# Attention through agents, then one expert per token: a first batch whose keys all come ahead of its values in float32, maxima without GpSimd, and an expert picked from a mean

## The chip, the cores and the metric

The kernel runs on one core of one Trainium2 chip. The metric is the time of the whole program on the device in microseconds (us), lower is better: the median of 3 runs, 1204.39 us for the kernel before (1203.04 to 1204.79). A core has TensorE (PE in the profile; PEld is its weight loads), VectorE (DVE), ScalarE (ACT), GpSimd (POOL) and SyncE (SP, which here only starts DMAs). Each takes its instructions in order, and semaphores hold one engine until another is done.

## The reference

Four batches of 11,456 tokens with 128 features, and 49 agents per batch. First the agents look at all keys, then each query looks at the 49 agents, and the result goes through the best of 8 experts:

```python
def sm(a, b):                               # scores, softmax
    s = scale * (a @ b.transpose(0, 2, 1))
    s = s - s.max(-1, keepdims=True)
    e = np.exp(s)
    return e / (e.sum(-1, keepdims=True) + 1e-09)
agent_v = sm(agents, k) @ v                 # 4 x 49 x 128
x = (sm(q, agents) @ agent_v).reshape(B * N, 128)
xn = x / (norm(x) + 1e-06); en = expert_emb / (norm(expert_emb) + 1e-06)
logits = xn @ en.T / tau                    # 8 experts
expert_idx = np.argmax(logits, axis=1)      # top 1
gate_w = softmax(logits)[chosen]
out[token] = gate_w * (np.maximum(x[token] @ w1[e], 0) @ w2[e])   # 128 -> 1024 -> 128
```

So the values of a batch can only be weighted once its keys have been scored, and no query of a batch gets to its expert before that batch's `agent_v` is done.

## The kernel before

A batch is cut into 12 units of 1,024 tokens (128 partitions by 8 chunks; the last unit has 2 chunks of 96 tokens). Scores have 49 columns per chunk.

**Precision.** PE multiplies f16 at full rate, so an f32 operand is split into a f16 high part and a f16 low part. `split` does it for a unit of keys or queries: ACT squares it for a scale (L284), then high and low parts are made. In the FFN phase `LO_BY` deals out the low part: for "d" ACT makes the high part (L291) and DVE the low part (L296); for "P" POOL makes the high part (L289) and DVE the low part; for "p" ACT makes the high part and POOL the low part in two instructions (L293, L294). A DMA transposes both (L299, issued by SP), and three products per chunk make the scores (L308 to L310). Half the key units of the first batch go another way, `k1_f32`: PE transposes the f32 unit itself (L356) and multiplies in f32 (L365).

**One batch.** `k1_unit` and `k1_f32` score keys and keep a running maximum in `m_run` (L342, L368). `k_max` reduces it on DVE (L399) and across the 128 partitions by `allred`, a partition_all_reduce on POOL (L135). `k2_unit` takes the exponential of the scores less the maximum (L382, L384) and multiplies with the values and a column of ones (`avp`, L388, 129 columns, f32). `av_chain` adds up (`foldp`, L424, L426) and leaves `avT` (L432), the agents' values. `q_unit` does the softmax of a query unit (L545 to L554), has its weights transposed by DMA (`tt`, L556) and multiplies them with `r_hi`, `r_lo` (L565, L566), which yields the logits of the experts.

**Experts.** Nearly all tokens of a batch choose the same expert. The kernel counts votes among the tokens of the batch's first query unit (`pick_expert`), loads that expert's weights (L529, L530), folds `agent_v` into `w1` (`gh`, `gl`) and runs the batch's feed-forward part (FFN) with it. Tokens that chose another expert are counted (`count_strays`, L135 again) and done apart at the end.

**FFN.** 23 tiles per batch of 512 tokens, 8 steps per tile, so 184 steps per batch and 736 in all. A step: `hp` from `tt` and `gh`, `gl` (L698, L699, 512 columns), ACT's relu to f16 (L702), DVE's low part `hl` (L703), and three products with `w2` per 128 tokens (L720 to L722). `ot` (L735) goes out by DMA (L741).

**Order.** `first` is the start of the program: `PAT` lists its work for batch 0 letter by letter (K and V units, m for `k_max`, q for a query unit, c for `av_chain`), and `AHEAD` says how many letters ahead loads are issued. Then the FFN loop runs, and between its steps the generators `keys` (keys and values of batches 1 to 3, in the windows `W_`, as shares of 184 steps: keys from, keys to, values from, values to) and `queries` put in the work of what is to come. A scheduler then sets each engine's order; SP's DMAs stand in the order of the code at the start.

Of the kernel before, what the change touches and what calls it, by code (L numbers as in the profile page):

```python
# [10 lines left out]
F16 = mybir.dt.float16  # L11
# [20 lines left out]
def kernel(ctx: ExitStack, tc: tile.TileContext, q, k, v, agents, emb, tau, w1, w2, out):  # L32
# [23 lines left out]

    LO_BY = {"k": "pdP", "q": "pP"}
    LAG = 4

# [8 lines left out]
    ld = ctx.enter_context(tc.tile_pool(name="ld", bufs=8))  # L68
# [51 lines left out]
    unit_load(k, "k", 0, 0)  # L120
    a_sb = sm.tile([A, B, C], F32, name="a_sb", tag="a_sb", bufs=1)
    sp.dma_start(out=a_sb, in_=agents.rearrange("b a c -> a b c"))
    unit_load(k, "k", 0, 1)
    ident = cst.tile([P, P], F32, name="ident")
    make_identity(nc, ident)
# [48 lines left out]
    def now_run(g):  # L174

        while True:
            try:
                next(g)
            except StopIteration as s:
                return s.value  # L180

# [3 lines left out]
    sga, isga = now_run(pow2(allred(amx, 1, "amxr"), 10, "sga"))  # L185
# [7 lines left out]
    eights = cst.tile([P, P], BF16, name="eights")  # L193
    half = cst.tile([P, GC], F32, name="half")
    iota_k = cst.tile([P, E], BF16, name="iota_k")
# [34 lines left out]
    def setup():  # L230
# [47 lines left out]
    def split(kind, b, u, g):  # L278
# [4 lines left out]
        xs = wk.tile([P, UJ, 2, D], F16, name=kind + "s", tag="xs", bufs=3)  # L283
# [14 lines left out]
        xT = wk.tile([P, 2 * UJ, P], F16, name=kind + "T", tag="xT", bufs=3)  # L298
# [15 lines left out]
    def k_start(b):  # L314
# [3 lines left out]
        for us in [range(x, y) for x, y in zip(e, e[1:])]:  # L318
# [3 lines left out]
            pool.memset(kb.m_run, -3.0e38)  # L322
# [5 lines left out]
    def k1_unit(b, u, g, cp):  # L328
# [8 lines left out]
        if cp is act:  # L337
            act.activation(st, spv, AF.Copy, scale=iv)
        else:
            dve.tensor_scalar(st, spv, iv, None, ALU.mult)  # L340
        yield g[2]
        dve.tensor_tensor(out=kb.m_run[:p, :n, :], in0=kb.m_run[:p, :n, :], in1=st, op=ALU.max)  # L342
        kb.s[u] = st
        kb.k1 += 1

    def k1_f32(b, u):
# [15 lines left out]
        yield 1  # L362
# [4 lines left out]
        act.activation(st, s[:p, : n * A].rearrange("p (c a) -> p c a", a=A), AF.Copy, scale=sga[:p])  # L367
        dve.tensor_tensor(out=kb.m_run[:p, :n, :], in0=kb.m_run[:p, :n, :], in1=st, op=ALU.max)  # L368
# [27 lines left out]
    def k_max(b, i=0):  # L396
# [3 lines left out]
        kb.m = allred(m1, A, "kmax", bufs=max(2, NB))  # L400
# [15 lines left out]
    def av_chain(b, g):  # L416
# [8 lines left out]
        for i, (x, m) in enumerate(fm):  # L425
# [8 lines left out]
                          in1=lr.unsqueeze(1).broadcast_to([P, 2, A]), op=ALU.mult)  # L434
        yield g
# [24 lines left out]
    def pick_expert(b, zo, g):  # L460
# [4 lines left out]
        n = ushape(0)[1]  # L465
        psx = pss if b else psh
        key = psx("key")
        for c in range(n):
            pe.matmul(out=key[:, :E], lhsT=eights, rhs=zo[:, c, :], start=(c == 0), stop=False)
        pe.matmul(out=key[:, :E], lhsT=eights, rhs=iota_k, start=False, stop=True)  # L470
        e0i = sm.tile([P, 1], I32, name="e0i", tag="e0i")
        dve.tensor_reduce(out=e0i, in_=key[:, :E], axis=AX.X, op=ALU.max)
        yield 1
# [4 lines left out]
        yield 5  # L478
        gh = wk.tile([P, F], F16, name="gh", tag="gh")
# [56 lines left out]
    def q_unit(b, u, g):  # L536
        bt = batches[b]
        p, n = ushape(u)
        while ("q", b, u) not in units:
            yield 1  # L540
        xT, iv = yield from split("q", b, u, g[0])
        yield g[1]
        spv = scores(b, u, xT)
# [12 lines left out]
        sp.dma_start_transpose(out=tt[:, : n * p].rearrange("k (c p) -> k c p", p=p),  # L556
                               in_=e2[:p, :n, :].rearrange("p c k -> p (c k)"))
# [553 lines left out]
```

## Time and profile before

| | |
|---|---|
| Median of 3 runs | 1204.39 us |
| Profiled execution: its time / span of the core | 1205.41 / 1203.6 us |
| Mean granted TensorE clock | 0.958 |
| Busy: PE / PEld / DVE / ACT / POOL | 86 / 70 / 75 / 57 / 36% |
| First FFN product (L698) starts | 109.56 us |
| L703 (`hl`, DVE) | 736 times, 475.5 us |
| L720, L721, L722 (PE) | 2880 times each, 222 ns mean |

The shares are means over the start (up to 110 us, no FFN) and the FFN phase. The page's slices show what a mean hides: a slice of 30 us with a low PE digit or a low clock digit has a wait in it.

### The profile page before, as it was taken

The page shows a single profiled execution, that of the slowest core. Times are in us where ns is not written, and L with a number is a line of the kernel's source. Part 1 is how long each engine was busy: PE and PEld are TensorE (multiplying, and loading weights), DVE is VectorE, ACT ScalarE, POOL GpSimd, SP SyncE. Part 2 cuts the span into 40 slices and gives each one's busy share as a digit, 9 for nine tenths or more (in the row PEclk, how much of TensorE's full clock was granted, in tenths as well). Part 3 has the DMA queues.
Part 4 walks back from the last instruction along what each step waited for, and adds up shares of the span by engine and source line. Part 5 has one row for each costly group of instructions (what it writes and reads, how often), then busy time and mean ns, then how long its engine had stood idle before and what let it go on. Part 6 is the DMA issues. An engine that isn't in the chain of part 4 may idle for free. (4 is left out here: it accounts for less than half of the span.)

```text
span 1203.6 us, 34100 instructions
## 1 busy us (share of the span) xinstructions
PE 1036.3 (86%) x13877; PEld 844.2 (70%) x13877; DVE 903.1 (75%) x2103; ACT 686.9 (57%) x1304; POOL 430.0 (36%) x409
## 2 busy tenths in 40 slices
PE   2666876698999877799998987689999989999998
PEld 2664655577787765587887776568788867877776
DVE  2555787567688896788778887686778998777785
ACT  2434676455647765555755676555554575655553
POOL 2002665445401644733442343733331262252200
PEclk9887898899999999899999999899999999999999
DMA  4976999465225988554542699753330382241100
GB/s 143 249 143 209 226 200 206 106 159 128 68 60 199 205 202 192 123 119 111 140 137 54 151 236 204 158 98 96 100 73 28 91 208 68 93 92 46 39 37 32
DMA packets 302697, 157.35 MB, mean 131 GB/s; under 512 B 227067, under 2 KB 279371, under 8 KB 302539
## 3 DMA queue, kind: packets, MB, share of 16 engines
q1 hardware_dynamic: 302475, 155.16, 54.4%
q8 instruction: 109, 1.79, 0.6%
q14 instruction: 49, 0.40, 0.1%
q0 software_dynamic: 64, 0.00, 0.0%
HBM read 75.80 MB, written 23.53 MB: 83 GB/s over the span
## 5 line engine op out<-in xcount | busy, mean ns | idle before, releaser
L703 DVE SCALAR_TENSOR_TENSOR hl<-hp,hh 128x512 f16<-128x512 f32 (+1 forms) x736 | 475.5, 666 | 95.9 <-ACT hh L702 86.2
L702 ACT ACTIVATE hh<-hp 128x512 f16<-128x512 f32 (+1 forms) x736 | 414.8, 584 | 217.0 <-PE yp L721 95.1
L720 PE MATMUL yp<-w2h,hh 128*128 128x128 f16 (+1 forms) x2880 | 528.5, 222 | 6.2 <-DVE ot L735 6.2
L721 PE MATMUL yp<-w2l,hh 128*128 128x128 f16 (+1 forms) x2880 | 529.0, 222 | 1.9 <-DVE w2l L516 1.9
L722 PE MATMUL yp<-w2h,hl 128*128 128x128 f16 (+1 forms) x2880 | 528.8, 222 | 0.0
L698 PE MATMUL hp<-tt,gh 128*128 128x512 f16 (+1 forms) x736 | 277.8, 378 | 66.1 <-DVE hl L703 60.4
L720 PEld LDWEIGHTS <-hh 128*128 128x128 f16 (+1 forms) x2880 | 288.0, 100 | 50.8 <-issue 3.3
L722 PEld LDWEIGHTS <-hl 128*128 128x128 f16 (+1 forms) x2880 | 287.8, 100 | 49.8 <-issue 6.2
L721 PEld LDWEIGHTS <-hh 128*128 128x128 f16 (+1 forms) x2880 | 288.1, 100 | 46.3 <-issue 8.5
L699 PE MATMUL hp<-tt,gl 128*128 128x512 f16 (+1 forms) x736 | 278.0, 378 | 0.3 <-DVE gl L507 0.3
L699 PEld LDWEIGHTS <-gl 128*128 128x128 f16 x736 | 72.0, 98 | 78.3 <-issue 73.1
L591 POOL TENSOR_TENSOR rt<-rt,qe 128x392 f32<-128x392 f32 (+1 forms) x48 | 49.7, 1036 | 158.6 <-ACT rt L590 158.6
L388 PE MATMUL avp<-vt,kd 128*98 128x129 f32 x720 | 98.1, 282 | 7.8 <-issue 7.8
L554 POOL TENSOR_TENSOR e<-qe,e 128x392 f16<-128x392 f32 (+1 forms) x48 | 41.7, 868 | 175.3 <-DVE e L553 134.6
L388 PEld LDWEIGHTS avp<-vt,kd 128*98 128x98 f32 x720 | 88.2, 170 | 14.0 <-issue 8.3
L284 ACT ACTIVATE qs<-qt 128x1024 f16<-128x1024 f32 (+1 forms) x48 | 48.2, 1005 | 62.0 <-DMA qt<-in_q_dram 29.4
L698 PEld LDWEIGHTS <-gh 128*128 128x128 f16 x736 | 72.4, 98 | 4.4 <-issue 0.7
L622 POOL TENSOR_TENSOR nrm<-quad,half 128x16 f32<-128x16 f32 (+2 forms) x28 | 68.3, 2440 | 2.2
L158 DVE TENSOR_SCALAR hsc<-usq 128x1 int32<-128x1 int32 x90 | 13.1, 147 | 73.4 <-ACT qs L284 50.3
L735 DVE TENSOR_TENSOR ot<-yp,gs 128x512 f32<-128x512 f32 (+1 forms) x92 | 61.4, 668 | 6.6 <-PE yp L722 6.5
L284 ACT ACTIVATE ks<-kt 128x1024 f16<-128x1024 f32 (+1 forms) x42 | 42.5, 1012 | 40.0 <-DMA kT<-ks 16.0
L384 ACT ACTIVATE kd<-kd,escale 128x392 f32<-128x392 f32 (+1 forms) x48 | 28.1, 597 | 61.3 <-POOL kd L382 54.6
(252 smaller groups left out, 1520.1 us busy)
## 6 DMA issues: line engine op xcount, KB each, us to landing
kt<-in_k_dram SPq DMA_DIRECT2D x44, 512.0 KB, 4.9
vt<-in_v_dram SPq DMA_DIRECT2D x44, 512.0 KB, 4.5
qt<-in_q_dram SPq DMA_DIRECT2D x44, 512.0 KB, 4.2
out_dram<-ot SPq DMA_DIRECT2D x88, 256.0 KB, 2.3
w1s<-in_moe_w_dram SPq DMA_DIRECT2D x5, 512.0 KB, 3.8
w2s<-in_moe_w_dram SPq DMA_DIRECT2D x5, 512.0 KB, 4.7
qT<-qs SPq DMA_TRANSPOSE x48, 4.7
tt<-e SPq DMA_TRANSPOSE x48, 3.4
```

Source lines behind the costliest of these rows:

```text
L284: act.activation(xs[:p, :n, 0], s[:p, :n], AF.Square, accum_out=sq)
L388: pe.matmul(out=avp[: 2 * A, :W], lhsT=de[:p, c * A : (c + 2) * A], rhs=src[:p, c, :], start=(c == 0), stop=(c == n - 1))
L591: pool.tensor_tensor(out=rt, in0=rt, in1=e, op=ALU.mult)
L622: pool.tensor_tensor(out=nrm, in0=quad[:, :n], in1=half[:, :n], op=ALU.pow)
L698: pe.matmul(out=hp[:, :m], lhsT=bt.gh[:, fs], rhs=tt, start=True, stop=False)
L699: pe.matmul(out=hp[:, :m], lhsT=bt.gl[:, fs], rhs=tt, start=False, stop=True)
L702: act.activation(hh[:, :m], hp[:, :m], AF.Relu)
L703: dve.scalar_tensor_tensor(out=hl[:, :m], in0=hp[:, :m], scalar=0.0, in1=hh[:, :m], op0=ALU.max, op1=ALU.subtract)
L720: pe.matmul(out=y, lhsT=hh[:, cs], rhs=bt.w2h[:, f, :], start=(f == 0 and c == 0), stop=False, skip_group_check=True)
L721: pe.matmul(out=y, lhsT=hh[:, cs], rhs=bt.w2l[:, f, :], start=False, stop=False, skip_group_check=True)
L722: pe.matmul(out=y, lhsT=hl[:, cs], rhs=bt.w2h[:, f, :], start=False, stop=last, skip_group_check=True)
L735: dve.tensor_tensor(out=o[:p, :n], in0=yp[:p, :n], in1=gate, op=ALU.mult)
```

## The change

1. *Start.* `ident` is made by DVE (a 32-column ramp, its 32x32 transpose, compared) and not by POOL's `make_identity`; the agents are loaded ahead of the first keys.
2. *Maxima over partitions.* `allmax` replaces `allred` everywhere: PE transposes the column, DVE reduces, PE spreads the result by a product with a broadcast operand, ACT copies it.
3. *First batch.* All 12 key units come first and all go through `k1_f32`; one `k_max`; then 12 value units. The first two query units also go in f32 over PE, their softmax weights transposed by PE (`ident16`). Both stand ahead of `av_chain` in the code.
4. *Expert.* `pick_expert` takes the mean row of `agent_v` (the sum of `avT` over agents times the experts' vectors, argmax) right after `avT`, not the votes of the first query unit.
5. *FFN phase.* Every split makes its high part on ACT and its low part with two POOL instructions (L300, L301 of the changed kernel). `run_max` takes the maximum straight from PSUM. Buffers: 5 instead of 3 for the split units and their transposes, 11 instead of 8 for loads. Windows `W_` of batches 2 and 3 begin earlier; generators wait longer between their parts.

```diff
-    LO_BY = {"k": "pdP", "q": "pP"}
+    XB = 5
-    ld = ctx.enter_context(tc.tile_pool(name="ld", bufs=8))
+    ld = ctx.enter_context(tc.tile_pool(name="ld", bufs=11))
...
-    make_identity(nc, ident)
+    i32 = sm.tile([P, 2, 32], F32, name="i32", tag="i32", bufs=1)
+    dve.memset(ident, 0.0)
+    dve.memset(i32[:, 0, :1], 0.0)
+    for w in (1, 2, 4, 8, 16):
+        dve.tensor_scalar(i32[:, 0, w : 2 * w], i32[:, 0, :w], float(w), None, ALU.add)
+    dve.transpose(out=i32[:, 1], in_=i32[:, 0])
+    for i in range(0, P, 32):
+        dve.tensor_scalar(ident[i : i + 32, i : i + 32], i32[i : i + 32, 0], i32[i : i + 32, 1, :1], None, ALU.is_equal)
...
-    def allred(col, n, tag, op=ROP.max, bufs=2):
+    def allmax(col, n, tag, psx, g, bufs=2):
+        t_ = psx("mT")
+        pe.transpose(out=t_[:n, :P], in_=col, identity=ident)
+        mx = sm.tile([P, 1], F32, name="mTx", tag="mTx")[:n]
+        dve.tensor_reduce(out=mx, in_=t_[:n, :P], axis=AX.X, op=ALU.max)
+        yield g
+        t_ = psx("mB")
+        pe.matmul(out=t_[:, :n], lhsT=mx.broadcast_to([n, P]), rhs=ident[:n, :n], start=True, stop=True)
         r = sm.tile([P, n], F32, name="pm", tag=tag, bufs=bufs)
-        pool.partition_all_reduce(r, col, P, op)
+        act.copy(r, t_[:, :n])
         return r
...
-        lo = LO_BY[kind][u % len(LO_BY[kind])] if ffn_at[0] is not None else "d"
-        if lo == "P":
-            pool.tensor_tensor(out=xs[:p, :n, 0], in0=s[:p, :n], in1=sc.unsqueeze(2).broadcast_to([p, n, D]), op=ALU.mult)
-        else:
-            act.activation(xs[:p, :n, 0], s[:p, :n], AF.Copy, scale=sc)
-        if lo == "p":
+        act.activation(xs[:p, :n, 0], s[:p, :n], AF.Copy, scale=sc)
+        if ffn_at[0] is not None:
             pool.tensor_tensor(out=s[:p, :n], in0=s[:p, :n], in1=sc.unsqueeze(2).broadcast_to([p, n, D]), op=ALU.mult)
             pool.tensor_tensor(out=xs[:p, :n, 1], in0=s[:p, :n], in1=xs[:p, :n, 0], op=ALU.subtract)
         else:
             dve.scalar_tensor_tensor(out=xs[:p, :n, 1], in0=s[:p, :n], scalar=sc, in1=xs[:p, :n, 0],
                                      op0=ALU.mult, op1=ALU.subtract)
...
+    def run_max(kb, spv, iv, p, n):
+        mr = kb.m_run[:p, :n, :]
+        if kb.k1 == 0:
+            dve.tensor_scalar(mr, spv, iv, None, ALU.mult)
+        else:
+            dve.scalar_tensor_tensor(out=mr, in0=spv, scalar=iv[:p], in1=mr, op0=ALU.mult, op1=ALU.max)
...
+        sav = sm.tile([P, 1], F32, name="sav", tag="sav")
+        dve.tensor_reduce(out=sav, in_=bt.avT[:, :A], axis=AX.X, op=ALU.add)
+        key = psx("key")[:, :E]
+        pe.matmul(out=key, lhsT=sav.broadcast_to([P, P]), rhs=enT, start=True, stop=True)
...
+        f32 = b == 0 and u < 2
+        if f32:
+            xT = pe_T(units["q", b, u], p, n)
...
+            for c in range(n):
+                pe.transpose(out=tp[:, c * p : (c + 1) * p], in_=e2[:p, c, :], identity=ident16[:p, :p])
+            act.copy(tt[:, : n * p], tp[:, : n * p])
...
-    PAT = "KKKKmKVKVKVKVmKVKVKVKVmqVVVVcqnqnnqnn"
-    AHEAD = 3
+    PAT = "K" * NU + "m" + "V" * NU + "q" * min(2, LEAD) + "c" + "q" * max(0, LEAD - 2) + "n" * min(5, NU)
+    AHEAD = 9
-    KF = [1, 3, 5, 7, 9, 11]
...
-        W_ = [(0, 0.2, 0.2, 0.7), (-0.2, 0.0, 0.3, 0.85), (-0.2, 0.0, 0.3, 0.85)]
+        W_ = [(0, 0.25, 0.3, 0.8), (-0.5, 0.25, 0.3, 0.8), (-0.5, 0.25, 0.3, 0.8)]
```

Three places show how the instructions move. First PE at the very start of the program: `aT` is the agents' transpose, `kTp` and `fTp` the f32 transposes of key units, `sp` the scores, `a_113` the agents in f16. Before:

```order
L129 MATMUL aT<-ident,a_sb 128x49 x4
L356 MATMUL kTp<-ident,kt 128x128 x8
L365 MATMUL sp<-aT_all,kT 128x49 x4
L356 MATMUL kTp<-ident,kt 128x128 x8
L365 MATMUL sp<-aT_all,kT 128x49 x4
L308 LDWEIGHTS kT
L308 MATMUL sp<-a_113,kT 128x49
```

And now, from the same place up to the first value product (`mT` and `mB` are `allmax`):

```order
L135 MATMUL aT<-ident,a_sb 128x49 x4
L362 MATMUL fTp<-ident,kt 128x128 x8
L149 MATMUL mT<-ident,amx 1x128
L362 MATMUL fTp<-ident,kt 128x128 x16
L154 MATMUL mB<-ident,mTx 128x1
L380 MATMUL sp<-aT_all,fT 128x49 x8
...
L380 MATMUL sp<-aT_all,fT 96x49 x2
L149 MATMUL mT<-ident,m_509 49x128
L154 MATMUL mB<-ident,mTx 128x49
L404 MATMUL avp<-vt,kd_143 98x129 x8
```

The f16 products that waited for a DMA transpose are gone from the first batch's keys, and all transposes and scores of its 12 units stand ahead of the first `avp`.

Second, PE at the end of the first batch's values (`e_0` and `e_1` are the softmax weights of the first two query units, `tp` their transpose). Before:

```order
L388 MATMUL avp<-vt,kd_130 98x129 x8
L388 MATMUL avp<-vt,kd_131 98x129 x2
L268 MATMUL embT<-ident,emb_sb 128x8
L424 MATMUL foldp<-wfold,avx 128x49
L426 MATMUL foldp<-wfold,avx 128x49 x3
```

Now:

```order
L404 MATMUL avp<-vt,kd_145 98x129 x2
L572 MATMUL sp<-aT_all,fT 128x49 x8
L594 LDWEIGHTS e_0_146
...
L362 MATMUL fTp<-ident,qt 128x128 x8
L572 MATMUL sp<-aT_all,fT 128x49 x4
L279 MATMUL embT<-ident,emb_sb 128x8
L572 MATMUL sp<-aT_all,fT 128x49 x4
L594 LDWEIGHTS e_1_147
...
L440 MATMUL foldp<-ident,avx 128x49
L442 MATMUL foldp<-ident,avx 128x49
```

The scores of both query units, and the transposes of their softmax weights, have moved ahead of `foldp`.

Third, POOL at the maximum of batch 1 (`pm` is the maximum over partitions, `kd` the scores less it, `rt` and `nrm` belong to query units). Before:

```order
L294 TENSOR_TENSOR qs_2521<-qt_2397,qs_2521 128x8x128
L111 MEMSET vt_3406 128x8
L135 ISA
L135 ISA pm_2667<-m1_2665 128x49
L322 MEMSET m_run_10820 128x392
L382 ISA
L382 TENSOR_TENSOR kd_0_129<-s_u_1161,pm_2667 128x392
```

Now:

```order
L301 TENSOR_TENSOR ks_4260<-kt_3931,ks_4260 128x8x128
L300 TENSOR_TENSOR qt_4014<-qt_4014,hsc_4603 96x256
L301 TENSOR_TENSOR qs_4569<-qt_4014,qs_4569 96x2x128
L109 MEMSET vt_4372 128x8
L623 TENSOR_TENSOR rt_2863<-rt_2863,qe_2664 128x392
L398 TENSOR_TENSOR kd_0_143<-s_u_1204,pm_2943 128x392
```

The two ISA rows on either side of the maximum are gone. Up to that `kd`, POOL had 22 instructions of L289, L293 and L294 before, and has 48 of L300 and L301 now. In the order now, PE's transpose for the maximum (`mT`) of batches 1, 2 and 3 stands behind 78, 243 and 427 of the 736 FFN steps.

## Rows read from the trace of the kernel before

**Rows 1.** Stretches, length; PE, PEld, DVE, ACT, POOL busy (count); clock; DMA share, GB/s.

```profile
110.00:222.00 112.00, 85.58 (x1268) 66.80 (x1267) 90.89 (x206) 76.11 (x141) 62.74 (x45) 0.92 0.98 215
222.00:240.00 18.00, 9.71 (x91) 7.49 (x90) 5.91 (x11) 5.88 (x11) 8.08 (x9) 0.72 0.32 76
400.00:476.00 76.00, 60.75 (x978) 49.74 (x978) 67.15 (x138) 50.63 (x99) 37.16 (x27) 0.96 0.89 191
...
680.00:746.00 66.00, 56.08 (x853) 44.70 (x852) 58.46 (x142) 47.04 (x94) 29.70 (x24) 0.95 1.05 236
...
764.00:1204.00 440.00, 416.29 (x5588) 335.98 (x5585) 343.81 (x795) 245.28 (x469) 125.87 (x114) 0.99 0.34 84
```

**Rows 2.** Timeline: start, length, engine, instruction, idle before and releaser; POOL and PE.

```profile
230.17 1.85 POOL L382 TENSOR_TENSOR kd<-s_u,pm 128x392 f32<-128x392 f32 x2 [7.73 <-issue]
...
233.03 0.58 PE L698 MATMUL hp<-tt,gh 128*128 128x512 f16 x1 [8.29 <-DVE hl L703]
...
488.68 0.59 PE L698 MATMUL hp<-tt,gh 128*128 128x512 f16 x1 [10.76 <-DVE hl L703]
...
758.06 0.59 PE L698 MATMUL hp<-tt,gh 128*128 128x512 f16 x1 [8.64 <-DVE hl L703]
```

**Rows 3.** Stretches, L703 alone (one per FFN step): DVE busy us (count), clock.

```profile
109.00:222.00 113.00, 38.64 (x59) 0.92 0.98 217
...
1040.00:1190.00 150.00, 82.70 (x124) 0.99 0.22 58
```

**Rows 4.** Timeline of the start: first key tile on ACT, identity on POOL.

```profile
4.14 1.06 ACT L284 ACTIVATE ks<-kt 128x1024 f16<-128x1024 f32 x1 [2.12 <-DMA kt<-in_k_dram]
...
13.99 0.28 POOL masks.py:199 TENSOR_SCALAR_AFFINE_SELECT ident<-ident 128x128 f32<-128x128 f32 x1 [12.14 <-issue]
```

**Rows 5.** Timeline of PE in the first batch: f32 transposes, scores, value products.

```profile
15.35 1.97 PE L356 MATMUL kTp<-ident,kt 128*128 128x128 f32 x8
...
30.38 3.63 PE L365 MATMUL sp<-aT_all,kT 128*128 128x49 f32 x16
...
47.44 3.65 PE L388 MATMUL avp<-vt,kd 128*98 128x129 f32 x16
...
51.96 1.99 PE L365 MATMUL sp<-aT_all,kT 128*128 128x49 f32 x16 [0.20 <-DVE avx L391]
...
60.68 1.94 PE L388 MATMUL avp<-vt,kd 128*98 128x129 f32 x16
...
70.22 3.73 PE L388 MATMUL avp<-vt,kd 128*98 128x129 f32 x16 [5.67 <-issue]
```

**Rows 6.** Timeline from the first query's softmax to the first FFN product.

```profile
90.63 0.57 DVE L545 TENSOR_REDUCE qmx<-sp 128x8 f32<-128x392 f32 x1 [1.00 <-PE sp L310]
...
93.28 0.42 PE L424 MATMUL foldp<-wfold,avx 49*128 49x49 f32 x2 [0.25 <-DVE avx L393]
...
94.05 1.23 SPq L556 DMA_TRANSPOSE tt<-e  x1
...
95.15 0.26 DVE L432 TENSOR_TENSOR avT<-foldp,lr 128x98 f32<-128x98 f32 x1
...
101.93 0.39 SPq L529 DMA_DIRECT2D w1s<-in_moe_w_dram  x1
...
109.56 0.38 PE L698 MATMUL hp<-tt,gh 128*128 128x512 f16 x1
```

**Rows 7.** Groups of POOL instructions: busy us, mean ns, idle before and releasers.

```profile
L622 POOL TENSOR_TENSOR nrm<-quad,half 128x16 f32<-128x16 f32 (+2 forms) x28 | 68.3, 2440 | 2.2
L294 POOL TENSOR_TENSOR qs<-qt,qs 128x1024 f16<-128x1024 f32 x23 | 51.6, 2242 | 1.0
L591 POOL TENSOR_TENSOR rt<-rt,qe 128x392 f32<-128x392 f32 (+1 forms) x48 | 49.7, 1036 | 158.6 <-ACT rt L590 158.6
```

**Rows 8.** Lines L293 and L296: duration ns min/median/max, first and last start.

```profile
L293 POOL TENSOR_TENSOR qt<-qt,hsc x23: 1882/1893/2897, 125.4 to 1062.5; 128x1024 f32<-128x1024 f32 x23
...
L296 DVE SCALAR_TENSOR_TENSOR qs<-qt,hsc,qs x25: 471/1276/3162, 74.7 to 1069.8; 128x1024 f16<-128x1024 f32 x21, 96x256 f16<-96x256 f32 x4
```

More of the change, by code (lines that the diff above doesn't have):

```diff
@@ L7 @@
 from concourse import bass_utils, mybir
-from concourse.masks import make_identity
 from concourse._compat import with_exitstack
@@ L172, in total @@
         return s
[L174 to L180, printed above, removed]
     amx = cst.tile([P, 1], F32, name="amx")
     dve.tensor_reduce(out=amx, in_=aT_all, axis=AX.XY, op=ALU.max, apply_absolute_value=True)
[L185 removed]
+    sga, isga = now_run(pow2(now_run(allmax(amx, 1, "amxr", pss, 0)), 10, "sga"))
     escale = cst.tile([P, 1], F32, name="escale")
@@ L282, in split @@
         sq = sm.tile([P, 1], F32, name="usq", tag=kind + "usq", bufs=3)[:p]
-        xs = wk.tile([P, UJ, 2, D], F16, name=kind + "s", tag="xs", bufs=3)
+        xs = wk.tile([P, UJ, 2, D], F16, name=kind + "s", tag="xs", bufs=XB)
         act.activation(xs[:p, :n, 0], s[:p, :n], AF.Square, accum_out=sq)
@@ L297, in split @@
                                      op0=ALU.mult, op1=ALU.subtract)
-        xT = wk.tile([P, 2 * UJ, P], F16, name=kind + "T", tag="xT", bufs=3)
+        xT = wk.tile([P, 2 * UJ, P], F16, name=kind + "T", tag="xT", bufs=XB)
         sp.dma_start_transpose(out=xT[:, : 2 * n, :p], in_=xs[:p, :n].rearrange("p c h d -> p (c h d)"))
@@ L361, in k1_f32 @@
                 act.copy(dst, tp[:, : m * p])
-        yield 1
+        return xT
+    def k1_f32(b, u):
+        kb = blk_of(b, u)
+        p, n = ushape(u)
+        while ("k", b, u) not in units:
+            yield 1
+        kT = pe_T(units["k", b, u], p, n)
+        yield 2
         s = pss("sp")
@@ L434, in av_chain @@
                           in1=lr.unsqueeze(1).broadcast_to([P, 2, A]), op=ALU.mult)
+        if b == 0:
+            bt.pick = pick_expert(b, 0)
+            next(bt.pick)
+        else:
+            spawn(pick_expert(b, 2), 1)
         yield g
@@ L464, in pick_expert @@
             yield 1
-        n = ushape(0)[1]
         psx = pss if b else psh
[L467 to L470, printed above, removed]
+        sav = sm.tile([P, 1], F32, name="sav", tag="sav")
+        dve.tensor_reduce(out=sav, in_=bt.avT[:, :A], axis=AX.X, op=ALU.add)
+        key = psx("key")[:, :E]
+        pe.matmul(out=key, lhsT=sav.broadcast_to([P, P]), rhs=enT, start=True, stop=True)
+        km = sm.tile([P, 1], F32, name="km", tag="km")
+        dve.tensor_reduce(out=km, in_=key, axis=AX.X, op=ALU.max)
+        ko = sm.tile([P, E], F32, name="ko", tag="ko")
+        dve.scalar_tensor_tensor(out=ko, in0=key, scalar=km, in1=iota8m, op0=ALU.is_ge, op1=ALU.mult)
         e0i = sm.tile([P, 1], I32, name="e0i", tag="e0i")
-        dve.tensor_reduce(out=e0i, in_=key[:, :E], axis=AX.X, op=ALU.max)
-        yield 1
+        dve.tensor_reduce(out=e0i, in_=ko, axis=AX.X, op=ALU.max)
         dve.tensor_scalar(e0i, e0i, E - 1, None, ALU.bitwise_and)
@@ L478, in pick_expert @@
         yield 5
+        while not hasattr(bt, "sg"):
+            yield 1
         gh = wk.tile([P, F], F16, name="gh", tag="gh")
@@ L540, in q_unit @@
             yield 1
-        xT, iv = yield from split("q", b, u, g[0])
-        yield g[1]
-        spv = scores(b, u, xT)
+        f32 = b == 0 and u < 2
+        if f32:
+            xT = pe_T(units["q", b, u], p, n)
+            yield 1
+            s = pss("sp")
+            for c in range(n):
+                pe.matmul(out=s[:p, c * A : (c + 1) * A], lhsT=xT[:, c * p : (c + 1) * p], rhs=aT_all[:, b, :], start=True, stop=True)
+            spv = s[:p, : n * A].rearrange("p (c a) -> p c a", a=A)
+            iv = SCALE
+        else:
+            xT, iv = yield from split("q", b, u, g[0])
+            yield g[1]
+            spv = scores(b, u, xT)
         mx = sm.tile([P, UJ], F32, name="qmx", tag="qmx")[:p, :n]
@@ L555, in q_unit @@
         tt = wk.tile([P, UJ * P], F16, name="tt", tag="tt", bufs=LEAD + 2)
-        sp.dma_start_transpose(out=tt[:, : n * p].rearrange("k (c p) -> k c p", p=p),
-                               in_=e2[:p, :n, :].rearrange("p c k -> p (c k)"))
+        if f32:
+            tp = psh("tp").bitcast(F16)
+            for c in range(n):
+                pe.transpose(out=tp[:, c * p : (c + 1) * p], in_=e2[:p, c, :], identity=ident16[:p, :p])
+            act.copy(tt[:, : n * p], tp[:, : n * p])
+        else:
+            sp.dma_start_transpose(out=tt[:, : n * p].rearrange("k (c p) -> k c p", p=p),
+                                   in_=e2[:p, :n, :].rearrange("p c k -> p (c k)"))
         yield g[4]
@@ L746, in count_strays @@
     def count_strays():
-        cur = allred(cnt_p, NG, "cntr")
+        cur = yield from allmax(cnt_p, NG, "cntr", pss, 1)
         yield 2
@@ L990, in first @@
                 q0[0] = iter(())
+                now_run(batches[0].pick)
             yield 1
@@ L1019, in keys @@
                         yield 1
-                    k_max(b)
-                    yield 2
+                    yield from k_max(b, pss, 1)
+                    yield 1
                 spawn(k2_unit(b, u, pool, (3, 4)))
```

69 lines of the change are left out of this document (28 added, 41 removed).

## The prediction, made before the changed kernel ran

> **What bounds the kernel now.** I read the busy shares and the 40 slices first, then the FFN phase cut into stretches, the timeline of POOL and PE where a stretch showed idle PE, and last the timeline of the start, from the first load to the first FFN product.
>
> The last 440 us are PE's: 416 of 440 busy at a clock of 0.99 [rows 1]. What is left to win in the FFN phase is ahead of that. From 110 to 222 us PE is idle for 26.4 us and the clock is 0.92; from 400 to 476 it is idle for 15.3, from 680 to 746 for 9.9 [rows 1]. These are the stretches in which the next batch's keys are split and scored, with the DMAs near their limit (share 0.89 to 1.05). Behind each stands a hole: PE waits 8.29, 10.76 and 8.64 us for `hl` [rows 2], which is 27.7 us, and the clock falls (0.72 in the first [rows 1]). Each hole begins at POOL's all-reduce, after which POOL issues nothing for 7.7 us [rows 2]. How much a step takes shows the same: 59 steps in 113 us, 1.9 us each, up to the first hole, and 124 in 150 us, 1.21 each, near the end [rows 3].
>
> The start is a chain of its own, as no FFN step can run before 109.56 us [rows 6].
>
> **The change, part by part.** The sum is made against the profiled execution, 1205.4 us (1.0 above the median).
>
> *First PE work.* POOL's identity is done at 14.3 us, after 12.1 us without an instruction, though a key tile had landed by 4.14 [rows 4]. DVE's thirteen short instructions need no load; bounds 4 and 8 us, I take 5, and 1.0 for the four transposes of the agents (14.3 to 15.35 before). PE begins on keys at 6.
>
> *Keys of batch 0.* A unit costs 1.97 us of transposes and 3.63 of scores in f32 [rows 5], 5.6 together, at the low level of TensorE's clock (1.2 GHz), and about 1.0 + 1.99 = 3.0 at the high one (2.4) [rows 5]. Which holds? Transposes ran at the low level at 15.35, and after 15 us in which PE did these two kinds and some f16 scores, with gaps, the scores at 30.38 still did. The high level first shows at 51.96, behind value products with their 129 columns, and after an idle time of 5.67 us value products are slow again (3.73, where they had been 1.94) [rows 5]. So I take the low level for all: 11 x 5.6 + 1.4 for the short unit = 63, and 1 for the first maximum: PE is through at 70.
>
> The Trainium skill ("TensorE: Matmul & The Clock Gate", Part 1) says that the throttle is the default and sustained activity releases it; an unbroken key phase would then end at the high level. By the rows above 15 us with gaps were not enough, and no run here shows 60 without; what it would give is a rival below.
>
> *Maximum.* Reduce, transpose, reduce, product, copy, subtraction, exponential: seven short steps between four engines. The nearest chain is a query's softmax, 90.63 to 94.05, 3.4 us [rows 6]; the all-reduce's 8 us is the other bound. I take 4.5: first `avp` at 74.5.
>
> *Values.* Twelve units at 1.94, two of them slow until the clock rises (+2.5), and the first query's transposes (1.0): 25. The last `avp` ends at 100, where it ended at 93 before [rows 6].
>
> *Two f32 query units ahead of `foldp`.* This is new on the path: PE takes its work in order, so `foldp` waits for both. Scores 2.0, softmax 3.4, transposes 0.6, next unit's transposes 1.0 and scores 2.0, softmax 3.4, transposes 0.6: 13 us, and 14 with some of it at the low level (16 if all). Before, the softmax lay beside value products. `foldp` starts at 114.
>
> *Expert.* `foldp` to `avT` took 1.9 us, `avT` to the weights' DMA 6.8, from there to the first FFN product 7.6 [rows 6]. Now the DMA follows `avT` over seven short steps instead of the first query's vote: 3 (bounds 2 and 6.8). FFN begins at 114 + 2 + 3 + 7.6 = 126.6, **17 us later**. The choice of expert cannot move more, since nearly all tokens of a batch choose one.
>
> *Holes.* No all-reduce is left in the FFN phase. PE's part in a maximum is two short products, and it does not wait between them: FFN steps stand there. The 27.7 us go, and some 5 of slow clock with them, less 3 for what takes their place: **-30** (bounds -20 and -35).
>
> *Bursts of batches 2 and 3.* Their key windows become 138 steps long from 37, and five buffers stand where three did: of 15.3 + 9.9 us of idle PE and the clock loss beside it I take **-15** (bounds 0 and -27).
>
> *Burst of batch 1.* Its window stays short, and here the split costs POOL more. Up to the first `kd` POOL has 48 large instructions where it had 22. At 1.9 and 2.24 us [rows 7, 8] they take 100 us, with about 18 of `nrm` and `rt` [rows 7] 119 us for 78 steps. PE's own work there is 85.6 us for 59 steps [rows 1], and 19 more at 1.21 make 109. So POOL sets the pace, though by little: 10 us lost where idle and low clock cost 35 before. I take half the difference, **-12** (bounds 0 and -24), as POOL starts late and its units queue behind each other.
>
> *Splits elsewhere.* Over the program POOL has 164 large instructions for 106, 58 more of 2.1 us, +122 us in all; POOL was busy for 126 of the last 440 us [rows 1], so outside the first burst they hide behind PE. If not, the rival below holds. DVE loses 55 instructions of about 1.3 us [rows 8], ACT gains 20 copies; neither bounds PE (DVE is 344 of 440 busy [rows 1]). For contention and longer latencies: **+4**.
>
> The Trainium skill ("GPSIMD Engine Reference", section 4.1) speaks against both moves: it wants elementwise work on VectorE, about 2x faster there, and reductions over partitions on GpSimd. On the first the trace agrees (1.3 us in one DVE instruction [rows 8] for 4.1 in two of POOL's), on the second it doesn't: POOL is out for 7.7 us [rows 2]. Going by the page alone, moving the maxima would gain nothing.
>
> Sum: 1205.4 + 17 - 30 - 15 - 12 + 4 = 1169.4, as a median **1168**.
>
> **The rivals.**
>
> *The clock rises in the key phase.* For it: PE has 60 us of work without a wait, and f32 scores at 51.96 ran at 1.99 [rows 5] once the level was high. Against: the low durations at 15.35 and 30.38. Keys then take 36 us instead of 63, FFN begins at 99.6, and the time is 1141.
>
> *The bursts stay as they are.* The idle PE of the bursts comes from the DMAs, which are near their limit there [rows 1], and the same bytes must come. Only the holes go: 1205.4 + 17 - 30, **1191** as a median. Against: over 138 steps the same bytes need a quarter of the rate.
>
> *POOL becomes the bound, and it is slower than before.* Place: the first 78 FFN steps, where PE's key scores stand in order between steps and wait for POOL's low parts. Instructions of this kind have taken up to 2.9 us on POOL and 3.16 on DVE [rows 8], when both work at once. At 3.0 us the 48 take 144, with the 18 others 162 us against PE's 109: 53 lost where 35 were, and 0.3 more per us for the clock, +23; late low parts take the gain of the other bursts and it is 17 - 30 + 23 = +10: 1215. It decides from 2.84 us per instruction, where the total is that of before. Against: medians lie at their minimum (1.88 and 1.89), `hl` was no longer up to 222 us (0.655 us, beside much POOL work) than near the end (0.667) [rows 3], and DVE has fewer large instructions now.
>
> **How the numbers follow.** Forecast 0.55, clock rises 0.20, bursts stay 0.12, POOL bounds 0.13. The forecast's own range is 1152 to 1186. For 8 in 10 the range goes down to 1135, which takes in most of the clock's rival, and up to 1204. About 0.2% is what a measurement of this kernel tells from no change. The first three cases are faster, but wide bounds on the holes and the start leave some of them near zero: faster 0.82, same 0.04, slower 0.14.
>
> **What would show it.** Right: f32 scores of the key phase at 3.6 us per unit and first `avp` near 75; PE waiting twice for about 3.4 us ahead of `foldp`; first FFN product near 127; no wait of 8 us in the FFN phase; POOL near full in the 115 us behind the FFN's start and PE idle there for some 10 to 20 us. Wrong: scores of 2.0 us before the first `avp`; PE idle as much as before in the bursts; POOL's low parts at 2.8 us or more; first FFN product past 150.

## The result, and the profile after

The changed kernel takes 1151.37 us (median of 4 runs, 1144.93 to 1155.05), the kernel before on the same chip 1203.72. The ratio is 0.957, interval 0.952 to 0.962: 52 us faster, where 36 were forecast. The profiled execution took 1149.93 us, its span 1148.1.

Where the time came from is seen best at a few fixed points: the first `hl` of an FFN step, and those of steps 78, 243, 427 and 736. These are the stretches between them, before (from 111.7 us on), with the columns of [rows 1]:

```profile
111.70:261.60 149.90, 114.58 (x1617) 91.27 (x1616) 112.10 (x244) 91.31 (x170) 79.28 (x62) 0.91 0.86 189
261.60:519.30 257.70, 222.67 (x3108) 179.99 (x3106) 207.63 (x466) 159.74 (x303) 110.81 (x93) 0.97 0.62 148
519.30:801.80 282.50, 249.94 (x3470) 202.93 (x3468) 221.31 (x502) 169.57 (x327) 114.30 (x102) 0.98 0.61 142
801.80:1196.30 394.50, 384.10 (x5131) 310.90 (x5127) 314.12 (x736) 225.20 (x430) 108.36 (x98) 0.99 0.31 78
```

and after (from 100.9 us on):

```profile
100.90:228.20 127.30, 102.34 (x1522) 80.29 (x1522) 99.93 (x223) 96.35 (x173) 104.31 (x71) 0.92 0.96 210
228.20:474.10 245.90, 227.16 (x3173) 184.42 (x3172) 198.57 (x474) 170.71 (x325) 150.99 (x124) 0.99 0.70 170
474.10:744.00 269.90, 250.78 (x3445) 202.90 (x3444) 206.12 (x477) 171.18 (x325) 129.93 (x112) 0.97 0.60 140
744.00:1140.10 396.10, 384.88 (x5128) 310.98 (x5126) 308.62 (x715) 230.54 (x437) 115.48 (x99) 0.99 0.26 71
```

The start gives 10.8 us, the first 78 steps 22.6, the next two stretches 11.8 and 12.6, and the last loses 1.6. PE's idle time in the four stretches (length less PE busy) falls from 113 to 74 us; the length of each stretch times what its clock lacks falls from 31 to 25. So the 45 us of the FFN phase are idle PE, for the most part; PE's busy time falls by only 6.

PE's timeline of the start is the answer to [rows 5, 6]:

```profile
7.10 1.97 PE L362 MATMUL fTp<-ident,kt 128*128 128x128 f32 x8
...
9.08 2.74 PE L362 MATMUL fTp<-ident,kt 128*128 128x128 f32 x16
...
33.07 1.89 PE L380 MATMUL sp<-aT_all,fT 128*128 128x49 f32 x16
...
34.97 4.04 PE L380 MATMUL sp<-aT_all,fT 128*128 128x49 f32 x36
...
44.28 11.03 PE L404 MATMUL avp<-vt,kd 128*98 128x129 f32 x80 [1.66 <-issue]
...
67.19 1.99 PE L572 MATMUL sp<-aT_all,fT 128*128 128x49 f32 x16
72.47 1.03 PE L594 MATMUL tp<-ident,e 128*128 128x128 f16 x8 [3.29 <-POOL e L589]
...
80.89 1.03 PE L594 MATMUL tp<-ident,e 128*128 128x128 f16 x8 [3.28 <-POOL e L589]
81.85 0.66 PE L440 MATMUL foldp<-ident,avx 49*128 49x49 f32 x2
...
96.16 0.38 PE L730 MATMUL hp<-tt,gh 128*128 128x512 f16 x1
```

Sixteen transposes at 9.08 take 2.74 us where the eight ahead of them took 1.97: the clock rises within them. (The trace's record of the clock begins with this rise, at 10.8 us. Ahead of its first record the clock column shows 1.00, as it does in the kernel before at 30.38 us, where scores took 3.63; the level is read there from the durations.) From then on a unit's scores take 1.9 us, not 3.6, and the first value product runs at 44, not at 75. The two waits of 3.3 us ahead of `foldp` are there as forecast, and the first FFN product comes at 96.16.

What PE waits for in the FFN phase (line waited for: us in total, times, longest), before:

```profile
PE hp L698 <- DVE hl L703: 60.4, 32, 10.8
```

and after:

```profile
PE hp L730 <- DVE hl L735: 27.6, 30, 3.9
PE yp L752 <- DVE ot L767: 12.2, 2, 11.2
PE rtp L606 <- DMA tt<-e: 11.3, 14, 2.1
```

The three long waits of [rows 2] are gone. One of 11.2 us is new. It lies in the first burst, and the timeline of POOL, DVE and PE shows how it comes about:

```profile
146.20 0.25 POOL L649 TENSOR_SCALAR quad<-quad 128x16 f32<-128x16 f32 x1
...
150.21 2.14 POOL L301 TENSOR_TENSOR ks<-kt,ks 128x1024 f16<-128x1024 f32 x1
...
153.27 2.94 POOL L654 TENSOR_TENSOR nrm<-quad,half 128x16 f32<-128x16 f32 x1
...
158.26 2.14 POOL L301 TENSOR_TENSOR qs<-qt,qs 128x1024 f16<-128x1024 f32 x1
158.59 5.55 DVE L656 SCALAR_TENSOR_TENSOR nrm<-l,sg,nrm 128x16 f32<-128x16 f32 x1
160.35 3.75 POOL L300 TENSOR_TENSOR kt<-kt,hsc 128x1024 f32<-128x1024 f32 x2
...
170.09 1.29 DVE L767 TENSOR_TENSOR ot<-yp,gs 128x512 f32<-128x512 f32 x2
...
170.84 0.27 PE L752 MATMUL yp<-w2h,hh 128*128 128x128 f16 x1 [11.18 <-DVE ot L767]
```

POOL works without a gap from 109.7 to 164.1 us. The gate of a pair of query units (`quad`, `nrm`, then `gs`) stands in its queue behind low parts: `quad` is done at 146.45, and `nrm`, the next step, starts at 153.27, behind three of their instructions and a product of the next unit. A second delay is on DVE: L656, the step after `nrm`, takes 5.55 us where its median is 0.227, and ends at 164.14, 0.04 us after POOL's row. PE stops at 159.7. The rest of the gate, on DVE and ACT, takes 6 us more. `ot` needs the gate, and PE needs the PSUM that `ot` frees.

### The profile page after: what moved, and what is told of

It reads as the page before. It is cut to its first block, busy times and chain, and to the rows that moved or that the text cites. A ratio compares the mean times of both kernels' runs of the same rounds, so it can differ in the third digit from the quotient of the medians.

```text
span 1148.1 us, 34052 instructions
## 1 busy us (share of the span) xinstructions
PE 1044.0 (91%) x13878; PEld 851.4 (74%) x13878; DVE 865.7 (75%) x2043; ACT 705.9 (61%) x1330; POOL 517.0 (45%) x449
## 5 line engine op out<-in xcount | busy, mean ns | idle before, releaser
L752 PEld LDWEIGHTS <-hh 128*128 128x128 f16 (+1 forms) x2880 | 286.0, 99 | 56.9 <-ACT hh L734 10.3
L753 PEld LDWEIGHTS <-hh 128*128 128x128 f16 (+1 forms) x2880 | 286.3, 99 | 54.2 <-issue 14.7
L300 POOL TENSOR_TENSOR qt<-qt,hsc 128x1024 f32<-128x1024 f32 (+1 forms) x46 | 83.0, 1807 | 88.8 <-ACT qs L298 83.9
L404 PE MATMUL avp<-vt,kd 128*98 128x129 f32 x720 | 94.2, 279 | 3.3 <-issue 1.7
L301 POOL TENSOR_TENSOR qs<-qt,qs 128x1024 f16<-128x1024 f32 (+1 forms) x46 | 93.3, 2032 | 0.8
L300 POOL TENSOR_TENSOR kt<-kt,hsc 128x1024 f32<-128x1024 f32 (+1 forms) x36 | 64.3, 1791 | 30.6 <-ACT ks L298 30.6
L301 POOL TENSOR_TENSOR ks<-kt,ks 128x1024 f16<-128x1024 f32 (+1 forms) x36 | 72.3, 2011 | 0.7
```

The lines of the kernel that those rows point to most:

```text
L404: pe.matmul(out=avp[: 2 * A, :W], lhsT=de[:p, c * A : (c + 2) * A], rhs=src[:p, c, :], start=(c == 0), stop=(c == n - 1))
L752: pe.matmul(out=y, lhsT=hh[:, cs], rhs=bt.w2h[:, f, :], start=(f == 0 and c == 0), stop=False, skip_group_check=True)
L753: pe.matmul(out=y, lhsT=hh[:, cs], rhs=bt.w2l[:, f, :], start=False, stop=False, skip_group_check=True)
```

## The experiments

Medians are of 5 runs or more, but for the run on the clock (e8), which is one; the kernel before stood at 1203 to 1204 us in every set. Stretches are read from one profiled execution each. Those of the changed kernel were profiled twice, here and in run e12: the second took 251.9 us where it had taken 245.9, so a few us in one stretch show nothing.

**The holes.** The maxima alone, put into the kernel before, and taken out of the changed one:

```diff
# e1: before.py, k_max
-        kb.m = allred(m1, A, "kmax", bufs=max(2, NB))
+        if b > 0:
...
+            pe.transpose(out=t_[:A, :P], in_=m1, identity=ident)
+            dve.tensor_reduce(out=mx, in_=t_[:A, :P], axis=AX.X, op=ALU.max)
+            pe.matmul(out=t_[:, :A], lhsT=mx.broadcast_to([A, P]), rhs=ident[:A, :A], start=True, stop=True)
+            act.copy(kb.m, t_[:, :A])
# e2: after.py, k_max
+        if b > 0:
+            pool.partition_all_reduce(kb.m, m1, P, ROP.max)
+            yield g
+        else:
             kb.m = yield from allmax(m1, A, "kmax", psx, g, bufs=max(2, NB))
```

> The kernel before with one edit: the maxima over partitions of batches 1 to 3 go over PE, DVE and ACT, not POOL's all-reduce. Theory (the three holes are the all-reduce): PE's waits of 8.3, 10.8 and 8.6 us for hl at these places go, nothing of 5 us or more takes their place, and the time falls from 1204 by 25 to 33 us to 1171 to 1179. Rival (the holes are the piled-up work of the bursts, and PE would wait there anyway): PE still waits 5 us or more at two of the three places, and the time is 1192 to 1204.

> The changed kernel with one edit: batches 1 to 3 take their maximum by POOL's all-reduce again. Theory: three holes of 8 to 11 us come back, with the slow clock behind them; the time rises from 1151 to 1176 to 1184. Rival (with five buffers and longer windows the FFN has enough work ready to run through them): POOL is out for 7.7 us, PE is not, 1151 to 1160.

Measured: 1178.71 us for the first (ratio to before 0.979, 0.976 to 0.982), 25 us gained; 1175.61 for the second (0.976, 0.974 to 0.979), 24 lost against 1151.37. In the first the longest wait for `hl` is 4.2 us:

```profile
PE hp L708 <- DVE hl L713: 37.2, 39, 4.2
```

In the second three waits are back, here ahead of `hp` and `yp`, of 5.96, 7.2 and 7.0 us (a timeline row and rows of the waits in two stretches):

```profile
237.46 0.59 PE L735 MATMUL hp<-tt,gh 128*128 128x512 f16 x1 [5.96 <-DVE hl L740]
```

```profile
PE yp L757 <- ACT hh L739: 7.2, 1, 7.2
...
PE hp L735 <- DVE hl L740: 7.0, 1, 7.0
```

The theory holds from both sides: the all-reduces cost 24 to 25 us, at the lower edge of what was expected or just below it.

**The start.** The first batch in its old order, in the changed kernel:

```diff
-    PAT = "K" * NU + "m" + "V" * NU + "q" * min(2, LEAD) + "c" + "q" * max(0, LEAD - 2) + "n" * min(5, NU)
-    AHEAD = 9
+    PAT = "KKKKmKVKVKVKVmKVKVKVKVmqVVVVcqnqnnqnn"
+    AHEAD = 3
+    KF = [1, 3, 5, 7, 9, 11]
...
-        f32 = b == 0 and u < 2
+        f32 = False
...
-                spawn(k1_f32(b, u) if b == 0 else k1_unit(b, u, (0, 1)))
+                spawn(k1_f32(b, u) if b == 0 and u in KF else k1_unit(b, u, (0, 1)))
```

> The changed kernel with the order of the first batch as before: PAT, AHEAD 3, half the key units in f32, the rest split, no query unit in f32. Theory (the start is worth what its trace shows): first FFN product near 109 us where it is 96, and the time 1151 + 13 = 1164, 1160 to 1169. Rival (a later FFN start is made good, as more of batch 1 is ready by then): 1149 to 1156.

Measured: 1167.81 us (0.970, 0.966 to 0.974), as the theory said, but not for its reason. The first FFN product comes at 98.1 us, only 2 us later than with the new order:

```profile
L730 PE MATMUL hp<-tt,gh x736: 242/379/634, 98.1 to 1151.3; 128*128 128x512 f16 x176, 128*128 128x192 f16 x8
```

So most of the earlier FFN start (109.56 before) is not the f32 order's; it is that of what this run kept: the identity by DVE, no all-reduce on POOL in the start, the expert from the mean row, in shares that no run here tells apart. The loss lies in the first 78 steps, which take 149.9 us instead of 127.3 at a clock of 0.85; the profiled execution, 1162.09 us, is 12 us longer than the changed kernel's, so some 11 of these 23 us come back behind them:

```profile
101.90:251.80 149.90, 109.78 (x1597) 86.78 (x1597) 105.28 (x246) 108.05 (x194) 119.75 (x82) 0.85 0.98 208
```

PE waits there for the transposed weights of query units that are late, and again for `ot`:

```profile
PE rtp L606 <- DMA tt<-e: 19.4, 2, 12.3
PE yp L752 <- DVE ot L767: 7.9, 1, 7.9
```

The edit changes the order, the way of half the keys and that of the first query units at once, and which of them makes these units late it does not tell. It does answer a question on the clock: with the old order the scores run at the low level again, at 24 us still, and the trace's record of the clock begins with a rise at 37.6 us.

```profile
24.03 3.65 PE L380 MATMUL sp<-aT_all,fT 128*128 128x49 f32 x16 [3.08 <-DVE m_run L339]
```

**The two query units ahead of `foldp`.** They are put in after the sixth value unit:

```diff
-    PAT = "K" * NU + "m" + "V" * NU + "q" * min(2, LEAD) + "c" + "q" * max(0, LEAD - 2) + "n" * min(5, NU)
+    PAT = "K" * NU + "m" + "V" * (NU - 6) + "q" * min(2, LEAD) + "V" * 6 + "c" + "q" * max(0, LEAD - 2) + "n" * min(5, NU)
...
         if f32:
+            yield 5
             tp = psh("tp").bitcast(F16)
```

> The changed kernel with the first two query units put in after the sixth of the twelve value units, and their weights' transposes 5 half steps later, so that both softmaxes lie beside value products. Theory (the 14.7 us between the last value product and foldp are on the path, 6.6 of them pure waits): foldp starts within 2 us of the last value product, first FFN product at 88 us, time 1143 (1139 to 1147). Rival (the experts' weights or the burst behind the start set the pace): first FFN product at 94 to 97 or the time at 1149 to 1153 in spite of an earlier one.

Measured: 1139.19 us (0.947, 0.944 to 0.950), 12 less than the changed kernel. The transposes of the weights now stand between value products, without a wait, and `foldp` follows the last of these at once:

```profile
66.54 0.33 PE L595 MATMUL tp<-ident,e 128*128 128x128 f16 x3
...
68.51 0.50 PE L595 MATMUL tp<-ident,e 128*128 128x128 f16 x6
68.84 2.41 PE L404 MATMUL avp<-vt,kd 128*98 128x129 f32 x20
...
71.63 0.42 PE L440 MATMUL foldp<-ident,avx 49*128 49x49 f32 x2 [0.22 <-DVE avx L409]
```

The first FFN product comes at 86.1 us, 10 earlier, and the time keeps it all. The theory holds; what it missed is that PE, no longer idle, also kept the high clock (six transposes in 0.50 us, where eight took 1.03).

**POOL's share of the splits.** The old deal of the low parts, and a smaller step, every other key unit of batch 1 on DVE:

```diff
# e5: after.py, split, as the kernel before has it
+    LO_BY = {"k": "pdP", "q": "pP"}
...
+        lo = LO_BY[kind][u % len(LO_BY[kind])] if ffn_at[0] is not None else "d"
# e6: after.py, split
-        if ffn_at[0] is not None:
+        if ffn_at[0] is not None and not ((kind, b) == ("k", 1) and u % 2):
```

> The changed kernel with the old deal of the split's low parts (LO_BY): POOL has 30 large instructions up to batch 1's first kd where the changed kernel has 48, DVE has 23 more low parts there and 48 more over the program. Theory (POOL sets the pace of the first 78 steps): the idle PE from 150 to 170 us falls from 14.5 to under 6, and the time from 1151 to 1141 (1137 to 1146). Rival (DVE's added 1.3 us pieces delay hl and the gate values by as much): 1149 to 1158, with PE idle for as long, elsewhere.

> The changed kernel, where every other key unit of batch 1 alone has its low part from DVE in one instruction: 39 large POOL instructions up to batch 1's first kd, 6 more on DVE. Theory (POOL's queue makes the hole at 150 to 170 us): the hole falls under 6 us and the time to 1143 (1139 to 1148), from the first 78 steps alone. Rival (the hole is made by the gate's chain on DVE, not by the length of POOL's queue): hole as before, 1149 to 1154.

Measured: 1145.97 us (0.951, 0.948 to 0.953) and 1150.67 (0.956, 0.953 to 0.958), against 1151.37 and, run again with the last set, 1152.93 (0.957, 0.954 to 0.961). The old deal is some 6 us better, which its interval hardly parts from the changed kernel's. PE's idle time from 150 to 170 us falls from 14.5 to 5.3 us, as the theory said. Yet the first 78 steps take no less time, neither here (in an execution of 1154.95 us, the slowest of the six) nor with the queries beside the values (e10, which has the old deal in the first burst, against e4):

```profile
104.10:232.70 128.60, 105.12 (x1543) 81.91 (x1543) 115.44 (x244) 92.48 (x171) 80.69 (x58) 0.96 1.03 226
```

```profile
93.80:220.80 127.00, 106.93 (x1534) 83.67 (x1534) 113.61 (x239) 92.86 (x171) 80.37 (x57) 0.93 0.95 218
```

```profile
92.80:220.00 127.20, 107.03 (x1505) 82.92 (x1505) 98.69 (x219) 95.63 (x173) 101.70 (x69) 0.90 0.93 203
```

POOL is busy for 24 and 21 us less in them, DVE for 15 us more, and the length stays. So closing the hole did not shorten the burst, and that POOL sets its pace is not shown. Whether DVE takes over, or the DMAs set the pace (share 0.93 to 1.03), no run tells apart.

With half the keys on DVE the long wait is gone and 78 steps take 120.4 us instead of 127.3, but the next stretch takes 257.1 where it took 245.9 (251.9 when run again):

```profile
103.10:223.50 120.40, 103.40 (x1489) 80.40 (x1487) 102.80 (x228) 97.30 (x174) 87.11 (x59) 0.94 1.04 227
223.50:480.60 257.10, 229.43 (x3204) 185.88 (x3205) 201.22 (x475) 169.04 (x324) 150.30 (x124) 0.99 0.67 160
```

So the hole was found and its worth was wrong: the gain is given back behind the burst, PE idle for 28 us there and not 19 (24 when run again). Why, this run does not show.

**The windows.** W_ as before:

```diff
-        W_ = [(0, 0.25, 0.3, 0.8), (-0.5, 0.25, 0.3, 0.8), (-0.5, 0.25, 0.3, 0.8)]
+        W_ = [(0, 0.2, 0.2, 0.7), (-0.2, 0.0, 0.3, 0.85), (-0.2, 0.0, 0.3, 0.85)]
```

> The changed kernel with the windows W_ of before: keys of batches 2 and 3 in 37 steps again, not 138. Theory (the longer windows gave nothing that the rest doesn't give, since in the changed kernel's trace the stages behind the first maximum gain just about the holes): 1148 to 1156. Rival (the prediction's: the longer windows are worth some 15 us): 1162 to 1170, with PE idle by 5 us or more above the changed kernel's ahead of each of the two maxima.

Measured: 1155.77 us (0.959, 0.956 to 0.961). That is at the theory's upper edge, and far from the rival's 15 us. The windows are worth 3 to 4 us, if anything, as the interval overlaps the changed kernel's.

**The clock.** Products of 49 columns behind the first eight of the keys' transposes, one run (1159.21 us):

```diff
+    pre = pss("pre")
+    for _ in range(24):
+        pe.matmul(out=pre[:, :A], lhsT=ident, rhs=aT_all[:, 0, :], start=True, stop=True)
     amx = cst.tile([P, 1], F32, name="amx")
```

> The changed kernel with 24 f32 products of 49 columns (48 records), their results unused, put in behind the first 8 transposes. Theory A (any unbroken work brings the clock up): they begin at 0.227 us each and fall to about 0.118 within this block. Theory B (f32 products of 49 columns are mostly weight loads and leave the clock low; it was the 24 transposes at the start that raised it): all 48 stay at 0.227 us, some 10.9 us, and the level rises only as transposes run again. The first value product comes 6 to 7 us later under A, 10 or more under B.

```profile
7.79 1.97 PE L365 MATMUL fTp<-ident,kt 128*128 128x128 f32 x8
9.55 10.31 PE L198 MATMUL pre<-aT_all,ident 128*128 128x49 f32 x48
...
19.87 3.37 PE L365 MATMUL fTp<-ident,kt 128*128 128x128 f32 x16
...
23.48 1.99 PE L383 MATMUL sp<-aT_all,fT 128*128 128x49 f32 x16
```

All 48 records take 0.215 us each, without a gap, and the level stays low for these 10.3 us. It rises within the 16 transposes behind them, and the same 49-column products then run at 0.12. The first value product comes at 57.50 us, 13 later. This is what theory B forecast, though not its reason: that weight loads are why such products leave the level low, this run does not show. Together with the old order above, it shows that in this kernel the order of the first units decides when the key phase gets the high level: it came within transposes on end, in the changed kernel and here, and not within 49-column products.

**Together.** The queries beside the values with the old deal (e9), and with that deal for the first burst alone (e10), whose edits are those above; and three buffers instead of five (e11), in the changed kernel; the changed kernel again (e12):

```diff
# e11
-    XB = 5
+    XB = 3
```

> The changed kernel with the first two query units beside the values and the old deal of the low parts (LO_BY) together. Theory (the two gains, 12 us at the start and 5 in the FFN phase, lie in different places and add): 1134 (1130 to 1138). Rival (with the FFN starting 10 us earlier the first burst is bound by loads and DMA transposes, not by POOL): 1138 to 1144.

> As the run before, but the old deal of the low parts only for keys of batch 1 and queries of batch 0, POOL's two instructions everywhere else. Theory (POOL sets the pace in the first burst alone): as good as the old deal everywhere or better, 1130 to 1137. Rival (a shorter first burst is given back in the next stage, as with half the keys on DVE): 1138 to 1143.

> The changed kernel with three buffers, not five, for the split units and their transposes (XB). Theory (the buffers are what took the idle PE out of the bursts, since the windows gave little): the FFN phase loses what the bursts gained, and the time is 1160 to 1170. Rival (the buffers matter as little as the windows; longer gaps in the generators and the lighter DVE did it): 1148 to 1156.

> The changed kernel once more, unaltered, as a level for the other runs on the same chip. Both theories: 1147 to 1155.

Measured: 1134.45 us (0.942, 0.938 to 0.946), 1140.48 (0.946, 0.942 to 0.949), 1134.92 (0.942, 0.939 to 0.945) and 1152.93. The first two gains add, as expected; the deal for the first burst alone gives nothing beyond the queries' 12 us, the time that its rival forecast, so the old deal's 5 us do not lie in the first burst. The third result is on neither side of its expectation: **three buffers are 18 us better than five**. Its first two stretches

```profile
103.50:226.90 123.40, 103.84 (x1493) 81.98 (x1492) 95.22 (x214) 93.13 (x164) 96.28 (x64) 0.90 0.89 204
226.90:467.10 240.20, 225.90 (x3199) 184.43 (x3198) 193.78 (x473) 169.12 (x323) 148.49 (x121) 0.99 0.66 167
```

against those of the changed kernel, run again:

```profile
101.00:229.90 128.90, 104.56 (x1521) 82.04 (x1521) 99.00 (x223) 96.06 (x173) 104.22 (x71) 0.91 0.95 207
229.90:481.80 251.90, 227.92 (x3175) 185.03 (x3173) 201.92 (x476) 170.65 (x325) 151.22 (x124) 0.99 0.69 166
```

have 19.6 and 14.3 us of idle PE (length less PE busy) where that has 24.3 and 24.0, and the longest wait for `ot` from 100 to 228 us halves, from 9.3 us (run again) to 4.7 (three buffers):

```profile
PE yp L752 <- DVE ot L767: 10.2, 2, 9.3
```

```profile
PE yp L752 <- DVE ot L767: 6.9, 2, 4.7
```

In the order of the changed kernel, 22 large POOL instructions stand ahead of the second gate's `nrm`; with three buffers it is 14, and `nrm` starts at 140.53 us where it started at 153.27. A unit that finds no buffer is not split yet, so the splits cannot run so far ahead of the gate. The first stretch gives 5.5 us of the 18 and the second 11.7; the queue was followed in the first alone, so the mechanism of the larger part is not shown. Three buffers together with the queries beside the values is what these runs point to next; no run has both.

Taken out of the changed kernel one at a time, the maxima are worth 24 us, the start 16 and the windows 3 to 4, while POOL's added share costs 6 and the added buffers 18: some 20 of the 52 us. The rest lies in parts that no run took out (the identity by DVE, the expert from the mean row, `run_max`, the 11 load buffers, the generators' longer waits) or in how the parts act on each other.

## Why the prediction was right or wrong

The time lies in the range (1135 to 1204) and the direction was right, but the forecast of 1168 is 17 us too slow, by errors against each other: the first FFN product came 30 us earlier than forecast (96.16, not 126.6), and behind it 42 us were gained, not 53. That they partly cancel is luck.

- *Keys of batch 0, "So I take the low level for all"*: this step failed. 63 us were taken; PE was through after 32, at 39 us (34.97 and 4.04 for the last scores). Scores of 2.0 us are the first of the prediction's own signs of being wrong. The rows of before on which it rested [rows 5] had transposes and 49-column products in turn, with gaps. The new order begins with 24 transposes on end, as the order rows ahead of the prediction show, and the clock rose within them; with the old order the level stays low (e3). That was the first rival, and its FFN start (99.6) is the measured one (96.16) within 4 us. The Trainium skill ("TensorE: Matmul & The Clock Gate", Part 1), by which sustained activity releases the throttle, pointed the right way, and yet 10.3 us of unbroken 49-column products did not release it here.
- *Value units and the two query units*: 25 and 14 us were forecast; from 44.28 to 67.19 with the queries' transposes it took 23, and from there to `foldp` 14.7. Right, and the e4 run, whose `foldp` comes 10 us earlier and whose time is 12 shorter, shows that the query units were on the path.
- *The other terms of the start* were a little short: PE began on keys at 7.1 us (6 forecast), the maximum took 5.3 (4.5), and `foldp` to the first FFN product 14.3 (12.6).
- *Holes, -30*: 24 and 25 us in two runs; a little too much. PE's waits for `hl` fall by 23 us in e1 (60.4 to 37.2), not by the 27.7 of the holes, as waits of up to 4.2 us are left; what the slow clock was worth, no run tells apart. The row of the Trainium skill ("GPSIMD Engine Reference", section 4.1) that sends reductions over partitions to GpSimd does not hold for this kernel, by the same two runs.
- *Burst of batch 1, -12*: compared with the e1 run, which has no holes either, the changed kernel's 127.3 us are 12.5 less:

```profile
110.20:250.00 139.80, 112.71 (x1628) 89.68 (x1627) 114.64 (x245) 91.94 (x172) 79.87 (x62) 0.94 0.92 201
```

  The size came out, but its step "POOL sets the pace" is not borne out, and the agreement is luck as far as these runs go. POOL is busy for 104 of the 127 us, not for 119, and with 21 to 24 us less of it the stretch is as long (e5, e10). With the old start it takes 149.9 us (e3). The forecast that no wait of 8 us would be left failed as well: POOL's queue holds a small instruction of the gate behind long ones, DVE's next step takes 5.55 us beside them, and PE waits 11.2 us.
- *Bursts of batches 2 and 3, -15*: this failed too. Compared with e1 (249.1 and 273.4 us), the two stretches gain 3.2 and 3.5, which two executions of the changed kernel differ by as well. The windows are worth 3 to 4 us at most, and the five buffers cost 18 over the program. The prediction had counted both as gains.
- *Contention, +4*: the last stretch loses 1.6 us, and gains 0.9 in the second profile (393.6 us). The rival by which POOL's instructions take 2.84 us or more did not come: medians are 1.89 and 2.13.

Sum of what was measured in the profiles: -10.8 at the start, -22.6, -11.8, -12.6 and +1.6 in the four stretches, and +0.7 behind them, together -55.5.

## What to carry to other kernels

Where a unit of work runs at one of two clock levels, look at what stands first in the engine's new order, not only at the kinds of instructions: here, with 24 transposes on end first, a unit's scores took 1.9 us for 3.6. That did not bring the FFN forward by much, as the old order shows: its first product came only 2 us later. Ask of each added buffer what it lets run ahead, and in which queue that then stands in front of something urgent; five for three cost 18 us here. When PE stands still in the middle of a stage, follow the small operations on the path: one that starts late without a wait ahead of it on its engine, or takes many times its median. But judge a cure by the length of the stage, and not by the hole: here the hole closed and the stage was as long.

## What the runs showed of the hardware that was not expected

- A DVE instruction on 128x16 elements (L656) took 5.55 us while POOL ran three large instructions beside it; its median over the program is 0.227. It ended within 0.05 us of the last of them. So did the long cases of three other runs, beside three such instructions each: 4.42 us when the kernel is run again (e12), 5.44 with the old windows (e7), 5.22 with the all-reduce (e2). With three buffers its worst case is 1.13. What in POOL's work holds it up, no run tells apart.

```profile
L656 DVE SCALAR_TENSOR_TENSOR nrm<-l,sg,nrm x28: 215/227/5546, 94.1 to 1092.6; 128x16 f32<-128x16 f32 x20, 128x8 f32<-128x8 f32 x4, 128x2 f32<-128x2 f32 x4
```

- A partition_all_reduce shows 0.52 us in the trace and costs 8 us each of the time, 24 to 25 for three.
- 49-column f32 products in an unbroken run of 10.3 us did not bring TensorE from 1.2 to 2.4 GHz; once it was there, in turn with transposes, they ran at 0.12 us a record and the level stayed.
